# Attention logits by column-tiled matmuls, softmax in their layout, probabilities through DRAM

## The chip, the cores and the metric

The kernel runs on one core of one Trainium2 chip. The metric is the device time of one execution in microseconds (us). The engines are called PE (TensorE), DVE (VectorE), ACT (ScalarE), POOL (GpSimd) and SP (SyncE, which issues all DMAs here). The "span" of a profile runs from the first to the last instruction of a core and is some 2 us shorter than the device time.

## The reference

One layer on x of 2048 x 512 in bf16: layernorm, then the sum of x, a local attention and a gated feed-forward network.

```python
# attention: 32 heads of 16; query s sees keys s, s-2, ..., s-14
logits = jnp.einsum("bhsd,bhswd->bhsw", q, kg) * scale      # 8 keys per query and head
logits = jnp.where(mask[None, None, :, :], logits, -1e9)
attn = softmax(logits, axis=-1)
o = jnp.einsum("bhsw,bhswd->bhsd", attn, vg)                # then @ wo
# feed-forward: 512 -> 1376 -> 512
h = gelu(xn @ w_gate) * (xn @ w_up);  ffn = h @ w_down
return x + attention(xn) + ffn
```

## The kernel before

The program is a graph of tasks. A list scheduler inside the kernel orders them on each engine from guessed durations and priorities, over four blocks of 512 tokens. Each block's attention is: Q, K, V matmuls; on DVE 8 products PROD = Q * shifted K (head dims on partitions); the sum over 16 dims of each head on PE; softmax on DVE and ACT; on DVE 8 products PVS of probabilities (PT) with shifted V (BS, loaded from a DRAM copy of V); the sum over keys on PE (called the PVS reduction); then the output matmuls, accumulated with those of the feed-forward network. In the profiles PS is PSUM, where matmuls leave their results; XIN is x as loaded, XN and xnT its normalized forms; GG (after gelu) and UU are the two feed-forward projections and HT their product; OT is the attention output; E is a selector of zeros and constants; wsrc is zeros for filler matmuls.

The logits used the products as the stationary operand, so that queries land on partitions:

```python
for jj in range(4):
    w = 2 * (3 - jj) + wq
    wp = wmap(w)
    for ti in range(4):
        col = 512 * lg[ti // 2].slot + (ti % 2) * 256 + wp * 32 + 8 * g
        ins = e.matmul(PS[:, col:col + 8],
                       lhsT=PROD[:, it.slot, jj, ti * 128:(ti + 1) * 128],
                       rhs=E8[:, :], start=True, stop=True)   # 16 of these per task, 32 tasks
# ... softmax over [128 queries, 2 tiles x 8 keys x 32 heads] ...
ins = e.transpose(PSB[:, c0:c0 + 128], PB[:, ...], ident[:, :])        # "tpp", 4 per task, 8 tasks
e.activation(out=PT[:, ...], in_=PSB[...], func=ACTF.Identity)         # "evp", 8 in all
```

The sum over keys was column-tiled already: four matmuls with a 32-column selector, side by side in the array.

```python
for half in range(2):
    for d4 in range(4):
        ins = e.matmul(PS[32 * d4:32 * d4 + 32, 512 * it.slot:512 * it.slot + 512],
                       lhsT=E4[:, :], rhs=PVS[:, itp.slot, half, d4, :],
                       start=(half == 0), stop=(half == 1), tile_position=(0, 32 * d4))
```

Of the kernel before, what the change touches and what calls it, by code (L numbers as in the profile page):

```python
# [69 lines left out]

class Item:
    _n = 0

    def __init__(self, name, pool=None, stream=None, slot=None, psum=False):
        self.name = name
        self.pool = pool
        self.stream = stream
        self.slot = slot
        self.psum = psum or (pool is not None and pool.psum)
        self.tasks = []  # L80
        self.nleft = 0
        self.w_all = None
        self.w_part = {}
        self.r_all = []
        self.r_part = {}
        self.eng_last = {}
        self.alloc_task = None
        self.prev_tasks = []
        Item._n += 1
        self.uid = Item._n  # L90
# [37 lines left out]
class Graph:  # L128
# [117 lines left out]
    def schedule(self, params=None, prior=None):  # L246
# [38 lines left out]
        def res_time(t):  # L285
# [5 lines left out]
            for its in need.values():  # L291
# [4 lines left out]
                for it in its:  # L296
                    cnt[it.stream] = cnt.get(it.stream, 0) + 1
                for st, c in cnt.items():
                    q = pool.quotas.get(st)
                    if q is not None and pool.in_use.get(st, 0) + c > q:  # L300
                        return False, 0.0
                fr = sorted(pool.free, key=lambda x: (x[0], x[1]))
# [3 lines left out]
        def drop(t):  # L306
# [10 lines left out]
            for it in t.items:  # L317
                it.nleft -= 1
                it.tasks.remove(t)
                if it.nleft == 0 and it.pool is not None and it.slot is not None:  # L320
                    avail = max([x.done for x in it.tasks] + [0.0])
                    it.pool.free.append((avail, it.slot, it))
                    it.pool.in_use[it.stream] -= 1
            return 1

        while nsched < ntot:
# [73 lines left out]
            for it in t.items:  # L400
                if it.pool is not None and it.slot is None:
                    pool = it.pool
                    fr = min(pool.free, key=lambda x: (x[0], x[1]))
                    pool.free.remove(fr)
                    it.slot = fr[1]
                    pool.in_use[it.stream] = pool.in_use.get(it.stream, 0) + 1
                    it.alloc_task = t
                    it.prev_tasks = [pt for pt in fr[2].tasks if pt is not t] if fr[2] is not None else []
                    if fr[2] is not None:
                        for pt in fr[2].tasks:  # L410
                            if pt is not t:
                                t.deps.add(pt)
# [35 lines left out]
            for it in t.items:  # L448
                it.nleft -= 1
                if it.nleft == 0 and it.pool is not None:  # L450
                    avail = max(x.done for x in it.tasks)
                    it.pool.free.append((avail, it.slot, it))
                    it.pool.in_use[it.stream] -= 1
# [177 lines left out]
def bass_parallel_sum__sliding_local_dilated__glu_gated_geglu__prompt_kernel(nc, A_x, A_wqkv, A_wo, B_x, B_w_gate, B_w_up, B_w_down, out, dbg=None, cfg=None):  # L631
# [4 lines left out]
    NPROD = cfg.get("NPROD", 3)  # L636
    NMS = cfg.get("NMS", 3)
# [4 lines left out]
    NEXPB = cfg.get("NEXPB", 4)  # L642
    NDE = cfg.get("NDE", 8 // NEXPB)
    NPB = cfg.get("NPB", 2)
# [20 lines left out]
    CHAIN_SHIFT = cfg.get("CHAIN_SHIFT", [0, 0, 0, 0])  # L665
# [10 lines left out]
    with contextlib.ExitStack() as es:  # L676
# [5 lines left out]
        Wqkv = sb("Wqkv", [128, 4, 1024], BF)  # L682
        WV = sb("WV", [128, 4, 512], BF)
# [4 lines left out]
        xnT = sb("xnT", [128, 4, S], BF)  # L688
# [3 lines left out]
        E8 = sb("E8", [128, 8], BF)  # L692
        E8f = sb("E8f", [128, 8], F32)
        E4 = sb("E4", [128, 32], BF)
        E4f = sb("E4f", [128, 32], F32)
        mask = sb("mask", [128, 512], F32)
# [10 lines left out]
        ms = sb("ms", [128, NMS, 3, 64], F32)  # L707
# [4 lines left out]
        DE = sb("DE", [128, NDE, 512], F32)  # L712
        PB = sb("PB", [128, NPB, 512], BF)
        PT = sb("PT", [128, NPT, 2, 512], BF)
# [10 lines left out]
        PSB = PS.bitcast(BF)  # L725
        VD = nc.dram_tensor("vt_scratch", (512, PITCH), BF, kind="Internal")
# [8 lines left out]
        P_xn = Pool("xn", NXN)  # L735
        P_qt = Pool("qt", NQT)
# [19 lines left out]
        I_xnT = Item("xnT")  # L756
# [18 lines left out]
        I_wv = Item("WV")  # L775
        I_VD = Item("VD")
        I_out = Item("out")

        def wmap(w):
            return (w % 2) * 4 + w // 2  # L780
# [14 lines left out]
            out=E8f[:, :], in_=E8f[:, :], pattern=[[-16, 8]], compare_op=ALU.is_ge, fill=0.0, base=0,  # L795
            channel_multiplier=1), rd=[I_E8f], wr=[I_E8f], prio=PC2)
        G.task("pool", "c_e8c", 0.25, lambda e: e.affine_select(
            out=E8f[:, :], in_=E8f[:, :], pattern=[[16, 8]], compare_op=ALU.is_ge, fill=0.0, base=15,
# [13 lines left out]
        G.task("pool", "c_mask0", 0.7, lambda e: e.memset(mask[:, :], 0.0), wr=[I_mask], prio=PC2)  # L812
        for w in range(1, 8):
            def mk(w=w):
                wp = wmap(w)
                return lambda e: e.affine_select(
                    out=mask[:, wp * 32:(wp + 1) * 32], in_=mask[:, wp * 32:(wp + 1) * 32],
                    pattern=[[0, 32]], compare_op=ALU.is_ge, fill=-1.0e9, base=-2 * w, channel_multiplier=1)
            G.task("pool", "c_mask%d" % w, 0.3, mk(), rd=[I_mask], wr=[I_mask], prio=PC2 + 10)
# [20 lines left out]
        for i, nm in enumerate(("q", "k")):  # L840
# [5 lines left out]
        it_wvraw = Item("wvraw", P_ot, "ot")  # L846
        G.task("sp", "ld_wv", 0, lambda e: e.dma_start(
            OT[:, it_wvraw.slot, :, :], A_wqkv[:, 1024:1536].rearrange("(k p) n -> p k n", p=128)),
            wr=[it_wvraw], prio=-898, nbytes=512 * 1024)
        permv_tasks = []  # L850
        for kt in range(4):
            def mk(kt=kt):
                return lambda e: e.activation(
                    out=WV[:, kt, :].rearrange("q (d h) -> q d h", d=16),
                    in_=OT[:, it_wvraw.slot, kt, :].rearrange("q (h d) -> q d h", d=16), func=ACTF.Identity)
            permv_tasks.append(G.task("act", "permv%d" % kt, 1.0, mk(), rd=[it_wvraw], wr=[(I_wv, kt)],
                                      prio=13))
# [27 lines left out]
        XINI = []  # L885
        for p in range(NP):
# [98 lines left out]
            def mk_ev(p=p, it=it_tp):  # L985
                return lambda e: e.activation(  # L986
                    out=xnT[:, :, 256 * p:256 * p + 256],
                    in_=PSB[:, 1024 * it.slot:1024 * it.slot + 1024].rearrange("q (k c) -> q k c", k=4),
                    func=ACTF.Identity)
            t_evx = G.task("act", "evx%d" % p, d_act(1024), mk_ev(), rd=[it_tp], wr=[(I_xnT, p)], prio=base + 6)  # L990
            if p == 1:
                for t_pv in permv_tasks:
                    G.order_after(t_pv, t_evx)

        QTI = []
        exp_pairs_per_batch = NP // NEXPB
        for b in range(NB):
# [7 lines left out]
            for hf in range(nh):  # L1005
                xparts = [(I_xnT, 2 * b), (I_xnT, 2 * b + 1)] if nh == 1 else [(I_xnT, 2 * b + hf)]
                hb = base + (10 * hf if nh > 1 else 0)
                for which in range(3):
                    for g in range(4):
                        it_mm = Item("mm%d_%d_%d_%d" % (b, which, g, hf), P_ps, "qkv")  # L1010

                        def mk_mm(which=which, g=g, it=it_mm, c0=c0b + hf * HWD, HWD=HWD):
                            def f(e):
                                ins = None
                                for kt in range(4):
                                    if which < 2:
                                        lhsT = Wqkv[:, kt, which * 512 + g * 128:which * 512 + (g + 1) * 128]
                                    else:
                                        lhsT = WV[:, kt, g * 128:(g + 1) * 128]
                                    ins = e.matmul(PS[:, 512 * it.slot:512 * it.slot + HWD], lhsT=lhsT,  # L1020
                                                   rhs=xnT[:, kt, c0:c0 + HWD], start=(kt == 0), stop=(kt == 3))
# [3 lines left out]
                               rd=xparts + [(I_wq, "qk"[which]) if which < 2 else I_wv],  # L1025
# [17 lines left out]
                        else:  # L1043
# [7 lines left out]
                            def mk_s(g=g, it=it_vt[g][hf], c0=c0b + hf * HWD, HWD=HWD):  # L1051
                                return lambda e: e.dma_start(
                                    bass.AP(VD, g * 128 * PITCH + 16 + c0, [[PITCH, 128], [1, HWD]]),
# [4 lines left out]
            it_lg = [Item("lg%d_%d" % (b, h), P_ps, "lg") for h in range(2)]  # L1058
            for g in range(4):
                for wq in range(2):  # L1060
                    it_pr = Item("pr%d_%d_%d" % (b, wq, g), P_prod, "p")

# [11 lines left out]
                    def mk_r(wq=wq, g=g, it=it_pr, lg=it_lg):  # L1074
                        def f(e):
                            ins = None
                            for jj in range(4):
                                w = 2 * (3 - jj) + wq
                                wp = wmap(w)
                                for ti in range(4):  # L1080
                                    col = 512 * lg[ti // 2].slot + (ti % 2) * 256 + wp * 32 + 8 * g
                                    ins = e.matmul(PS[:, col:col + 8],  # L1082
                                                   lhsT=PROD[:, it.slot, jj, ti * 128:(ti + 1) * 128],
                                                   rhs=E8[:, :], start=True, stop=True)
                            return ins
                        return f
                    G.task("pe", "er%d_%d_%d" % (b, wq, g), d_mm(8, 16) + 0.06, mk_r(),
                           rd=[it_pr, I_E8], wr=[(it_lg[0], (wq, g)), (it_lg[1], (wq, g))], prio=base + 5, mode="f",
                           util=0.06)

            it_pt = Item("pt%d" % b, P_pt, "pt")
            for h2 in range(2):
                P = 2 * b + h2
                lg = it_lg[h2]
                batch = P // exp_pairs_per_batch
                it_de = Item("de%d" % P, P_de, "de")
                it_pb = Item("pb%d" % P, P_pb, "pb")
                it_ms = Item("ms%d" % P, P_ms, "ms")

                def lgv(lg=lg):  # L1100
# [318 lines left out]
```

## Time and profile before

The median was 214.04 us when the prediction was made, and 213.5 us in the groups of runs below.

| | PE | DVE | ACT |
|---|---|---|---|
| busy, us | 204.6 | 148.2 | 115.2 |
| share of the span | 97% | 70% | 54% |

The slices and the chain of waits are in the prediction. In the chain a piece "0.86 PE ... x4" is four matmuls of 512 columns issued 0.216 us apart.

### The profile page before, as it was taken

Reading aid. Unit: us, or ns where it says so; the run is one execution under the profiler, and the core shown is the slowest. Engines: PE = TensorE matmul, PEld = TensorE weight load, DVE = VectorE, ACT = ScalarE, POOL = GpSimd, SP = SyncE. Lnnn points to the kernel's source line nnn. Section 1 sums busy time; section 2 is a strip of 40 time slices with the busy share of each in tenths; the row PEclk is TensorE's granted clock in tenths of the full one; section 3 lists DMA queues with packets and bytes.
Section 4 is the critical chain, followed back from the end, with each engine's and each line's share of the span. In section 5 each row is a group of like instructions: output and inputs, shape, how many; then the busy total and the mean of one; then the engine's idle time right before and its main releaser. Section 6 shows DMA issues by size and latency. Waiting matters only on the chain.

```text
span 211.4 us, 3916 instructions
## 1 busy us (share of the span) xinstructions
PE 204.6 (97%) x1578; PEld 103.3 (49%) x1578; DVE 148.2 (70%) x239; ACT 115.2 (54%) x190; POOL 12.8 (6%) x44
## 2 busy tenths in 40 slices
PE   7799999999999999999999999999999999998994
PEld 2345565454444664544444654444445554443483
DVE  4508999999998597699822687698531887797121
ACT  2398767987810169976720149877400459848000
POOL 6701010010013000000000000000000000000000
PEclk9999999999999999999999999999999999999999
DMA  5999969023059610012012349140013258040021
GB/s 168 378 394 362 241 162 247 1 56 98 25 171 232 180 45 0 0 37 68 0 40 62 101 142 224 36 100 3 0 50 99 58 170 216 11 100 0 28 87 37
DMA packets 23777, 23.40 MB, mean 111 GB/s; under 512 B 2672, under 2 KB 22736, under 8 KB 23760
## 3 DMA queue, kind: packets, MB, share of 16 engines
q1 hardware_dynamic: 23760, 23.16, 38.4%
q8 instruction: 12, 0.20, 0.4%
q14 instruction: 5, 0.04, 0.1%
HBM read 18.94 MB, written 4.21 MB: 109 GB/s over the span
## 4 chain that ended last, share of the span: by engine, by line
PE 87%; DVE 7%; ACT 2%; DMA 1%; issue 1%; POOL 0%; ACTq 0%; DVEq 0%; POOLq 0%
PE PS L1242 32%; PE PS L1020 20%; PE PS L1289 18%; PE PS L1302 7%; PE PS L1082 6%; DVE PVS L1196 4%; PE PS L1211 3%; PE PS L978 2%; DVE st L907 1%; DMA XIN<-in_A_x_dram 1%; PE PS L1164 1%; DVE XN L965 1%; ACT PT L1173 1%; ACT xnT L986 0%; DVE HT L1264 0%
## 5 line engine op out<-in xcount | busy, mean ns | idle before, releaser
L1064 DVE TENSOR_TENSOR PROD<-QT,KT 128x2048 bf16<-128x2048 bf16 x32 | 37.3, 1219 | 11.5 <-ACT KT L1038 11.5
L1242 PE MATMUL PS<-xnT,Wu 128*128 128x512 bf16 (+1 forms) x176 | 45.2, 379 | 0.0
L1242 PE MATMUL PS<-xnT,Wg 128*128 128x512 bf16 (+1 forms) x176 | 45.1, 379 | 0.0
L1289 PE MATMUL PS<-Wd,HT 128*128 128x512 bf16 (+3 forms) x198 | 41.0, 356 | 0.2 <-ACT OT L1222 0.2
L1196 DVE TENSOR_TENSOR PVS<-BS,PT 128x2048 bf16<-128x2048 bf16 x32 | 37.0, 1220 | 3.6 <-ACT PT L1173 3.5
L1332 DVE TENSOR_TENSOR OB<-PS,XR 128x512 bf16<-128x512 f32 (+1 forms) x18 | 11.3, 630 | 31.9 <-PE PS L1302 31.8
L1020 PE MATMUL PS<-xnT,Wqkv 128*128 128x512 bf16 x128 | 30.3, 379 | 0.3 <-ACT xnT L986 0.3
L1252 ACT ACTIVATE GG<-PS 128x512 bf16<-128x512 f32 (+1 forms) x44 | 26.6, 604 | 6.4 <-PE PS L1242 6.1
L1259 ACT ACTIVATE UU<-PS 128x512 bf16<-128x512 f32 (+1 forms) x44 | 26.6, 604 | 4.6 <-PE PS L1242 4.4
L1289 PEld LDWEIGHTS PS<-Wd,HT 128*128 128x128 bf16 (+1 forms) x198 | 19.2, 98 | 19.1 <-ACT OT L1222 0.6
L1045 ACT ACTIVATE VT<-PS 128x512 bf16<-128x512 f32 x16 | 9.6, 598 | 34.4 <-PE PS L1020 34.4
L1242 PEld LDWEIGHTS PS<-xnT,Wu 128*128 128x128 bf16 (+1 forms) x176 | 16.9, 100 | 18.7 <-ACT QT L1031 0.4
L1242 PEld LDWEIGHTS PS<-xnT,Wg 128*128 128x128 bf16 (+1 forms) x176 | 17.0, 100 | 18.1
L1020 PEld LDWEIGHTS PS<-xnT,Wqkv 128*128 128x128 bf16 x128 | 11.9, 98 | 15.9 <-ACT KT L1038 0.8
L1038 ACT ACTIVATE KT<-PS 128x512 bf16<-128x512 f32 x16 | 9.6, 598 | 18.5 <-PE PS L1020 18.5
L1264 DVE TENSOR_TENSOR HT<-GG,UU 128x512 bf16<-128x512 bf16 (+1 forms) x44 | 16.8, 420 | 2.2 <-ACT UU L1259 2.2
L1082 PEld LDWEIGHTS PS<-E,PROD 128*128 128x128 bf16 x512 | 15.8, 96 | 4.5
L1302 PE MATMUL PS<-Wo,OT 128*128 128x512 bf16 (+1 forms) x72 | 16.8, 354 | 0.0
L1082 PE MATMUL PS<-E,PROD 128*128 128x8 bf16 x512 | 15.8, 166 | 0.0
L1020 PE MATMUL PS<-xnT,WV 128*128 128x512 bf16 x64 | 15.6, 378 | 0.0
L907 DVE BATCH_NORM_STATS2 st<-XIN 128x6 f32<-128x512 bf16 x16 | 10.7, 686 | 2.8 <-DMA XIN<-in_A_x_dram 2.8
L986 ACT ACTIVATE xnT<-PS 128x1024 bf16<-128x1024 bf16 x8 | 8.2, 1020 | 6.8 <-PE PS L978 6.8
(57 smaller groups left out, 147.1 us busy)
## 6 DMA issues: line engine op xcount, KB each, us to landing
BS<-vt_scratch SPq DMA_DIRECT2D x64, 128.5 KB, 3.4
XR<-in_A_x_dram SPq DMA_DIRECT2D x16, 128.0 KB, 2.2
vt_scratch<-VT SPq DMA_DIRECT2D x16, 128.0 KB, 1.7
XIN<-in_A_x_dram SPq DMA_DIRECT2D x7, 256.0 KB, 3.3
out_dram<-OB SPq DMA_DIRECT2D x14, 128.0 KB, 2.0
Wg<-in_B_w_gate_dram SPq DMA_DIRECT2D x1, 1376.0 KB, 9.5
Wu<-in_B_w_up_dram SPq DMA_DIRECT2D x1, 1376.0 KB, 12.5
Wd<-in_B_w_down_dram SPq DMA_DIRECT2D x1, 1280.0 KB, 9.8
```

Source lines behind the costliest of these rows:

```text
L907: return lambda e: e.bn_stats(out=st[:, t, :], in_=XIN[:, it.slot, t2, :])
L1020: ins = e.matmul(PS[:, 512 * it.slot:512 * it.slot + HWD], lhsT=lhsT, rhs=xnT[:, kt, c0:c0 + HWD], start=(kt == 0), stop=(kt == 3))
L1064: return lambda e: e.tensor_tensor(out=PROD[:, it.slot, :, :], in0=bass.AP(QT, (itq.slot * 4 + g) * 512, [[NQT * 4 * 512, 128], [0, 4], [1 ...
L1082: ins = e.matmul(PS[:, col:col + 8], lhsT=PROD[:, it.slot, jj, ti * 128:(ti + 1) * 128], rhs=E8[:, :], start=True, stop=True)
L1196: return lambda e: e.tensor_tensor(out=PVS[:, ito.slot, half, :, :], in0=BS[:, it.slot, :, o:o + 512], in1=bass.AP(PT, (itp.slot * 2 + hal ...
L1242: ins = e.matmul(PS[0:M, 512 * it.slot:512 * it.slot + 512], lhsT=Wx[:, kt, j * 128:j * 128 + M], rhs=xnT[:, kt, c0b:c0b + 512], start=(kt ...
L1252: return lambda e: e.activation(out=GG[0:M, ito.slot, :], in_=PS[0:M, 512 * it.slot:512 * it.slot + 512], func=ACTF.Gelu_apprx_tanh)
L1259: return lambda e: e.activation(out=UU[0:M, ito.slot, :], in_=PS[0:M, 512 * it.slot:512 * it.slot + 512], func=ACTF.Identity)
L1264: return lambda e: e.tensor_tensor(out=HT[0:M, ito.slot, j, :], in0=GG[0:M, ig.slot, :], in1=UU[0:M, iu.slot, :], op=ALU.mult)
L1289: ins = e.matmul(PS[:, 512 * it.slot:512 * it.slot + CW], lhsT=HT[0:K, ith.slot, j, ti * 128:(ti + 1) * 128], rhs=Wd[0:K, j, c0:c1], start ...
L1302: ins = e.matmul(PS[:, 512 * it.slot:512 * it.slot + CW], lhsT=OT[:, ito.slot, dq, ti * 128:(ti + 1) * 128], rhs=Wo[:, dq, c0:c1], start=F ...
L1332: return lambda e: e.tensor_tensor(out=OB[:, ito.slot, 0:CW], in0=PS[:, 512 * it.slot:512 * it.slot + CW], in1=XR[:, itx.slot, c0:c1], op= ...
```

## The change

The intent is to let PE stream the products through a small stationary selector, four query tiles at once, and not to load 512 blocks of products as weights for results of 8 columns. Logits then have heads on partitions, softmax runs in that layout, and the probabilities change to the layout of PVS by a store to DRAM and a load, which costs PE and ACT nothing. With it go other changes: V's permutation moves into the addresses of its store, so that WV need not be permuted on ACT; attention of later blocks gets a higher priority (CHAIN_SHIFT); xnT becomes three rotating buffers; PROD has four buffers for three. The core of the diff:

```diff
-    CHAIN_SHIFT = cfg.get("CHAIN_SHIFT", [0, 0, 0, 0])
+    CHAIN_SHIFT = cfg.get("CHAIN_SHIFT", [0, 300, 600, 900])
 ... (pools, buffers, mask, pairs of PSUM banks)
-                            for jj in range(4):
-                                ...
-                                    ins = e.matmul(PS[:, col:col + 8],
-                                                   lhsT=PROD[:, it.slot, jj, ti * 128:(ti + 1) * 128],
-                                                   rhs=E8[:, :], start=True, stop=True)
+                        for wq in range(2):
+                            for sj in range(4):
+                                ins = e.matmul(
+                                    PS[32 * sj:32 * sj + 32, 512 * (lg.slot + wq):512 * (lg.slot + wq) + 512],
+                                    lhsT=E8[:, 24 - 8 * g:56 - 8 * g],
+                                    rhs=PROD[:, prs[wq].slot, :, sj * 128:(sj + 1) * 128],
+                                    start=(g == 0), stop=(g == 3), tile_position=(0, 32 * sj))
 ... (softmax: the same steps, one of 1024 columns for two of 512)
-                G.task("pe", "tpp%d" % P, ...)      # transposes of the probabilities
-                G.task("act", "evp%d" % P, ...)     # and their eviction
+            for sj in range(4):                     # four stores ...
+                        bass.AP(PD, b * 128 * 1024 + sj * 256, [[1024, 32], [32 * 1024, 4], [1, 256]]),
+                        PB[32 * sj:32 * sj + 32, itp.slot, :].rearrange("q (j c) -> q j c", j=4))
+                    PT[:, it.slot, :], bass.AP(PD, b * 128 * 1024, [[1024, 128], [1, 1024]]))   # ... and a load
```

## The prediction

> **What bounds the kernel now.** I read the busy row and the 40 slices first. The slices show that TensorE (PE) is covered from the third slice to the 37th at full clock, while VectorE (DVE) and ScalarE (ACT) have holes.
>
> ```profile
> PE 204.6 (97%) x1578; PEld 103.3 (49%) x1578; DVE 148.2 (70%) x239; ACT 115.2 (54%) x190; POOL 12.8 (6%) x44
> PE   7799999999999999999999999999999999998994
> PEclk9999999999999999999999999999999999999999
> ```
>
> Busy TensorE time overlaps itself, because ends are modelled. I therefore read next the chain of waits in order of time, whose pieces on PE do not overlap. First the shares by line, from the page:
>
> ```profile
> PE 87%; DVE 7%; ACT 2%; DMA 1%; issue 1%; POOL 0%; ACTq 0%; DVEq 0%; POOLq 0%
> PE PS L1242 32%; PE PS L1020 20%; PE PS L1289 18%; PE PS L1302 7%; PE PS L1082 6%; DVE PVS L1196 4%; PE PS L1211 3%; PE PS L978 2%; DVE st L907 1%; DMA XIN<-in_A_x_dram 1%; PE PS L1164 1%; DVE XN L965 1%; ACT PT L1173 1%; ACT xnT L986 0%; DVE HT L1264 0%
> ```
>
> Then pieces of the chain (start, length, what):
>
> ```profile
> 10.93 7.08 PE PS L1020 x32
> 18.01 0.86 PE PS L1242 x4
> 18.88 0.38 PE PS L1082 x16
> ...
> 50.18 0.98 PE PS L1211 x16
> ...
> 71.34 1.18 PE PS L1082 x48
> ...
> 134.20 0.86 PE PS L1242 x4
> 135.06 0.22 PE PS L1164 x4
> ...
> 181.24 0.24 PE PS L1164 x4
> ```
>
> From 10.93 us to 181.5 us the chain is PE work laid end to end: four 512-column matmuls take 0.86 us, or 0.216 us each. After 181.5 us the chain leaves PE for the probabilities and PVS of the last block. That looks as if 13.6 us (181.5 to 195.1) were latency. The timeline of PE there says otherwise:
>
> ```profile
> 191.24 1.03 PE L1242 MATMUL PS<-xnT,Wu 128*96 128x512 bf16 x4
> 192.71 1.05 PE L1211 MATMUL PS<-PVS,E 128*32 128x512 bf16 x16 [0.44 <-ACT UU L1259]
> 193.69 1.25 PE L1362 MATMUL PS<-wsrc 128*128 128x512 bf16 x5
> 195.10 1.25 PE L1289 MATMUL PS<-Wd,HT 128*128 128x512 bf16 x5 [0.16 <-ACT OT L1222]
> ```
>
> PE still does feed-forward matmuls there until 192.1 us. Of the 3.0 us to 195.1 only 0.98 us is needed work (L1211); the L1362 fillers compute nothing. So about 2 us of the tail is lost, not 13.6. The kernel is a 10.9 us head, then about 184 us of needed PE issue time with 2 us lost near its end, 13.3 us of final accumulations, and about 3 us of output. **What leaves PE's stream shortens the time one for one, unless a new wait opens a hole in it.**
>
> **What the Trainium skill says.** "TensorE: Matmul & The Clock Gate", section Back-to-back issue gap, gives about 25 ns as the floor for 1 to 64 columns and N/2.4 + 2.5 ns for larger N. The trace agrees: 0.38 us for 16 matmuls of 8 columns is 24 ns each, and 512 columns take 216 ns. The old logits thus pay 16 issues and 16 weight loads for results of 8 columns.
>
> "TensorEngine Tiling (Array Packing)", section Key Properties, says that different tiles run weight loads and matmuls in parallel, and that a change of tiling mode drains TensorE. L1211 is already such a 128x32 matmul: 16 of them take 0.98 us, where four rounds of 0.216 are 0.86. So four do run at once, and a visit costs about 0.11 us extra.
>
> "SBUF — State Buffer", section Door 1, speaks of 16-byte lines, with a penalty for each access that crosses to a new line. The trace fits: the strided sum over SBUF takes 1038 ns for 512 elements (L1140), the same reduction from PSUM 685 ns (L1122).
>
> "DMA: Bandwidth & Descriptors", section Two DMAs through the same engine are not ordered, requires a wait for the first DMA's completion before a dependent one is issued. So the new path is two full trips in series. This trace has 128 KB stores to DRAM landing in 1.7 us, and loads of 128 to 256 KB in 2.2 to 3.4 us.
>
> **The change part by part.**
>
> Removed on PE: 32 logit tasks of 16 matmuls, at 0.38 to 0.39 us: 12.4 us. Also 8 transposes of probabilities (L1164) at 0.22: 1.8 us. Sum 14.2 us, all in the saturated stretch.
>
> Added on PE: 16 logit tasks of 8 column-tiled 512-column matmuls (four query tiles side by side, two PSUM banks, accumulated over the four head groups). In the order of the changed program they come as one visit of 16 and 14 of 8. By L1211's measure a visit of 8 costs 2 x 0.216 + 0.11 = 0.545 us; so 14 x 0.545 + 0.98 = 8.6 us. **Net on PE: minus 5.6 us.** All other matmul counts are unchanged in the order, apart from one more warm-up filler; the head stays bound by x, layernorm and the first transposes.
>
> ACT loses the permutation of WV (4.3 us) and the eviction of transposed probabilities (4.7 us), and about 0.5 us as four exponentials of 1024 columns replace eight of 512. ACT is not the bound: worth nothing directly.
>
> DVE: the softmax instructions now cost 8.0 + 4.9 + 4.5 + 4.5 + 3.8 + 1.0 + 0.7 + 0.7 = 28.1 us. The new ones per block: max, subtract and scale at about 1.2 us (twice 0.68 less one fixed part), sum about 2.0, reciprocal about 1.0, so four times 6.6 plus a small mask = 26.6 us. DVE is 1.5 us lighter, but in longer pieces. I expect PROD and PVS to keep their 1.22 us: the inner run of PVS becomes 128 elements, still contiguous bf16.
>
> Probabilities: before, a transpose of 0.22 and an eviction of 0.6 us. After, four stores issued at about 0.4 us, 1.7 us to land, one load of about 2.3 us: some 5.5 us from PB to PT, so 4 us more latency per block. The changed priorities move attention of later blocks ahead of feed-forward work to pay for this. In the new order the last block's second PVS reduction is followed by 13 feed-forward groups, so the roundtrip is out of the tail there. What stays at the end is the eviction and product of the last feed-forward tile, about 1.4 us from last matmul to first accumulation, against the 2 us lost now. Gain: 0.5 us.
>
> Do holes open in blocks 0 and 1? I walked the new order by hand with these durations. In block 0 the last logits end near 32.7 us, PB is ready near 42.5, PT near 48.4, and four PVS later (53 us) the first PVS reduction can start; PE arrives at 54.4. The second reduction is ready at 58.3, PE there at 58.5. That is tight, no hole. In block 1, counting from the end of block 0's accumulations, PB is ready at 16.5 us, PT at 22.0, DVE is free at 22.6, and the first reduction is ready at 27.2 while PE arrives at 26.9. The second must wait for four more PVS and two HT, 5.4 us, while PE has 4.4 us of other work: about 1 us. Block 2 has nearly 2 us of slack and block 3 more. I put 1.3 us on holes, with an uncertainty of 1.5 us.
>
> Sum: 214.04 - 5.6 - 0.5 + 1.3 = 209.2; I shade it to **209.0 us**, as the order is evidently laid out so that PE has other work near each wait.
>
> **The rivals.**
>
> First, DVE and the roundtrip become the bound in the first half. For it: DVE is busy 37.9 of 44 us between 11 and 55 us and 37.7 of 45 in the next stretch, and SyncE issues in order, so a store that waits for PB holds later loads. Against it: DVE's total falls, its second half is light (22.2 of 36.5 us from 145 to 181.5), and attention of block 0 had 4 us to spare before the accumulations. It would give back 3 to 6 us: 211 to 214.
>
> Second, no holes at all and a better tail: PE's saving comes through whole and the lost 2 us of the tail shrink by 1. For it: the kernel before has no PE hole above 0.5 us between 11 and 192 us, though its waits are similar. It would give 207.2 to 208.
>
> Third, column-tiled logits cost more than L1211's measure (each visit drains twice, or the strided reading of PROD is slower). At 0.8 us per visit instead of 0.545 the saving falls by 3.8 us: 212 to 213. Against it: L1211 has the same shape, contraction and stationary width.
>
> Fourth, the tail really was 13.6 us of latency and vanishes: 200 or less. Against it: the PE timeline above.
>
> **Range and chances.** The PE arithmetic alone gives 208; holes of 0 to 4 us lie on top, and 0.5 to 1 us may come from the tail. So 8 in 10 between 207.0 and 211.8. The 2% line is at 209.76, little above my centre: faster 0.60, within 2% 0.38, slower 0.02.
>
> **What would show it.** The column-tiled logits should fill about 8.6 us of the chain in pieces of 0.54 us; the line of probability transposes is gone; PVS stays at 1.22 us; the strided sum is near 2.0 us for 1024 elements; PT arrives about 5.5 us after PB. PE idle before the PVS reductions should total 0 to 3 us, mostly in blocks 0 and 1. The prediction is wrong if those waits exceed 4 us, if a logit visit costs over 0.7 us, if PVS falls out of its fast mode (8 us more on DVE for each 0.25 us), or if the span falls below 204 us.

## The result

The changed kernel took 210.09 us (median of 4; 210.00 to 210.33) against 213.74 us for the kernel before in the same group (213.40 to 214.10). The ratio of the fast runs is 0.9831, with a 95% interval from 0.9813 to 0.9849: 1.7% faster, within 2%. Ratios here and below are the mean time of one kernel's fast runs over that of the other's of the same rounds, so not quite the ratio of the medians quoted. The forecast range held; the centre of 209.0 was 1.1 us too low. Of the classes, the one given 0.60 (faster by more than 2%) did not come; "within 2%" had 0.38.

Busy times and slices of the changed kernel:

```profile
PE 200.5 (96%) x1142; PEld 90.6 (43%) x1163; DVE 147.9 (71%) x219; ACT 109.4 (53%) x174; POOL 11.4 (5%) x38
...
PE   7999999999989999999999999999999999999994
```

PE still covers nearly the whole span. (Of 1163 matmuls 1142 have a record; the count of weight loads is whole.) One slice has an 8, near 58 us. The chain of waits of the changed kernel, in the same columns as in the prediction:

```profile
26.05 0.55 PE PS L1083 x8
26.60 3.57 PE PS L1237 x16
...
104.64 0.98 PE PS L1206 x16
105.62 2.70 PE PS L1237 x12
...
190.82 0.60 ACT UU L1254
191.42 0.02 issue
191.45 0.43 DVE HT L1259
191.88 0.14 issue
192.01 2.54 PE PS L1284 x11
```

L1083 is the new logits line, L1206 the PVS reduction, L1237 the feed-forward line. A logit visit takes 0.55 us, as forecast. But look at what follows it: sixteen matmuls of 512 columns should take 16 x 0.216 = 3.46 us and take 3.57. The same holds after a PVS reduction, which is column-tiled too: twelve should take 2.59 and take 2.70. So **each visit also costs about 0.1 us after it**. The kernel before had the same 0.1 us after its PVS reductions (eight visits, unchanged: sixteen matmuls take 3.56), and only about 0.02 us after its old logits, which were not tiled (0.88 for 0.86). From its chain:

```profile
18.88 0.38 PE PS L1082 x16
19.26 0.88 PE PS L1242 x4
...
50.18 0.98 PE PS L1211 x16
51.16 3.56 PE PS L1020 x16
```

The chain goes by modelled ends. By starts the 0.1 us stands ahead of the visit and not behind it (this one starts at 25.98 us, where 25.88 was due); the sum is the same.

The final accumulations begin at 192.01 us against 195.10. From there on both kernels are equal (13.3 us to the last DVE step). All of the 3.1 us of span are gained before.

The timelines of PE where the 8 stands, of SP (issue of DMAs) ahead of it, and of DVE, in the changed kernel:

```profile
57.57 1.03 PE L1237 MATMUL PS<-xnT,Wg 128*128 128x512 bf16 x4
58.43 0.61 PE L986 MATMUL PS<-ident,XN 128*128 128x128 bf16 x8
59.98 1.05 PE L1206 MATMUL PS<-PVS,E 128*32 128x512 bf16 x16 [0.94 <-DVE PVS L1187]
```

```profile
43.10 0.78 SPq L1154 DMA_DIRECT2D pt_scratch<-PB  x2
43.98 0.40 SPq L907 DMA_DIRECT2D XIN<-in_A_x_dram  x1
44.42 0.96 SPq L1154 DMA_DIRECT2D pt_scratch<-PB  x2
47.40 0.34 SPq L1161 DMA_DIRECT2D PT<-pt_scratch  x1
```

```profile
41.79 1.23 DVE L1146 TENSOR_TENSOR PB<-DE,ms 128x1024 bf16<-128x1024 f32 x1
...
50.07 6.90 DVE L1187 TENSOR_TENSOR PVS<-BS,PT 128x2048 bf16<-128x2048 bf16 x6 [1.01 <-DMA PT<-pt_scratch]
```

PE waits 0.94 us for the last PVS products of block 0. The first began at 50.07 us, when PT landed; PB had been ready at 43.0. That is 7 us for the roundtrip, not the 5.5 forecast. A 256 KB load of x stands among the four stores, and PT's load is issued only when the last store has landed. It is the only large hole; block 1, where the prediction put 1 us, has none before its PVS reductions.

The softmax rows of the changed kernel, from the groups of instructions by form (busy us and mean ns after the count):

```profile
L1187 DVE TENSOR_TENSOR PVS<-BS,PT 128x2048 bf16<-128x2048 bf16 x32 | 37.3, 1217 | 3.6 <-DMA PT<-pt_scratch 2.6 <-PE PS L1206 1.0
L1138 DVE TENSOR_REDUCE ms<-DE 128x128 f32<-128x1024 f32 x4 | 7.7, 1914 | 2.5 <-ACT DE L1133 2.5
L1122 DVE TENSOR_REDUCE ms<-PS 128x128 f32<-128x1024 f32 x4 | 4.9, 1222 | 0.3 <-PE PS L1083 0.3
```

PVS kept its 1.22 us and the strided sum over SBUF takes 1.91 us, both as forecast. All softmax instructions on DVE come to 26.5 us, against 26.6 forecast.

My theory after this: PE's stream sets the time; each of the 16 logit visits costs about 0.21 us for going into column-tiled mode and coming back, of which the prediction counted half; and the late PT of block 0 costs about 1 us. The rivals: that the 0.1 us are an artefact of modelled ends; that DVE's load makes the hole; that ACT's lighter load was part of the gain.

### The profile page after: what moved, and what is told of

Same layout as the page of the kernel before. It is cut to its first block, busy times and chain, and to the rows that moved or that the text cites. A ratio compares the mean times of both kernels' runs of the same rounds, so it can differ in the third digit from the quotient of the medians.

```text
span 208.3 us, 3060 instructions
## 1 busy us (share of the span) xinstructions
PE 200.5 (96%) x1142; PEld 90.6 (43%) x1163; DVE 147.9 (71%) x219; ACT 109.4 (53%) x174; POOL 11.4 (5%) x38
## 4 chain that ended last, share of the span: by engine, by line
PE 90%; DVE 5%; issue 1%; DMA 1%; ACT 1%; POOL 0%; POOLq 0%; DVEq 0%
PE PS L1237 36%; PE PS L1021 19%; PE PS L1284 18%; PE PS L1297 7%; PE PS L1206 4%; PE PS L1083 3%; DVE st L915 2%; PE PS L986 1%; DVE PROD L1068 1%; DVE PVS L1187 1%; DMA XIN<-in_A_x_dram 1%; DVE XN L973 1%; ACT UU L1254 1%; PE PS L854 1%; POOL sq L930 0%
## 5 line engine op out<-in xcount | busy, mean ns | idle before, releaser
L1237 PE MATMUL PS<-xnT,Wu 128*128 128x512 bf16 (+1 forms) x170 | 44.4, 379 | 0.6 <-issue 0.3
L1237 PE MATMUL PS<-xnT,Wg 128*128 128x512 bf16 (+1 forms) x172 | 44.7, 379 | 0.3 <-ACT UU L1254 0.2
L1021 PE MATMUL PS<-xnT,Wqkv 128*128 128x512 bf16 x187 | 43.6, 379 | 0.4 <-DVE PROD L1068 0.2
L1247 ACT ACTIVATE GG<-PS 128x512 bf16<-128x512 f32 (+1 forms) x44 | 26.5, 603 | 12.1 <-PE PS L1237 10.7
L1254 ACT ACTIVATE UU<-PS 128x512 bf16<-128x512 f32 (+1 forms) x44 | 26.5, 602 | 6.0 <-PE PS L1237 5.8
L1021 PEld LDWEIGHTS PS<-xnT,Wqkv 128*128 128x128 bf16 x192 | 18.0, 98 | 24.5 <-issue 2.1
L1259 DVE TENSOR_TENSOR HT<-GG,UU 128x512 bf16<-128x512 bf16 (+1 forms) x44 | 17.2, 417 | 13.3 <-ACT UU L1254 13.2
L1237 PEld LDWEIGHTS PS<-xnT,Wu 128*128 128x128 bf16 (+1 forms) x176 | 17.1, 100 | 21.7 <-ACT GG L1247 2.1
L1237 PEld LDWEIGHTS PS<-xnT,Wg 128*128 128x128 bf16 (+1 forms) x176 | 16.9, 100 | 21.2 <-issue 2.5
L1032 ACT ACTIVATE QT<-PS 128x512 bf16<-128x512 f32 x16 | 9.3, 595 | 27.7 <-PE PS L1021 27.7
L1217 ACT ACTIVATE OT<-PS 128x512 bf16<-128x512 f32 x16 | 8.7, 594 | 16.4 <-PE PS L1206 16.4
L994 ACT ACTIVATE xnT<-PS 128x1024 bf16<-128x1024 bf16 x8 | 8.2, 1024 | 8.6 <-PE PS L986 8.6
L1083 PE MATMUL PS<-PROD,E 128*32 128x512 bf16 x128 | 9.8, 384 | 0.2 <-PE PS L1083 0.2
## 6 DMA issues: line engine op xcount, KB each, us to landing
Wg<-in_B_w_gate_dram SPq DMA_DIRECT2D x1, 1376.0 KB, 10.5
```

Source lines behind the costliest of these rows:

```text
L1021: ins = e.matmul(PS[:, 512 * it.slot:512 * it.slot + HWD], lhsT=lhsT, rhs=xnT[:, itx.slot, kt, c0:c0 + HWD], start=(kt == 0), stop=(kt == 3))
L1083: ins = e.matmul(PS[32 * sj:32 * sj + 32, 512 * (lg.slot + wq):512 * (lg.slot + wq) + 512], lhsT=E8[:, 24 - 8 * g:56 - 8 * g], rhs=PROD[:, ...
L1237: ins = e.matmul(PS[0:M, 512 * it.slot:512 * it.slot + 512], lhsT=Wx[:, kt, j * 128:j * 128 + M], rhs=xnT[:, itx.slot, kt, :], start=(kt = ...
L1247: return lambda e: e.activation(out=GG[0:M, ito.slot, :], in_=PS[0:M, 512 * it.slot:512 * it.slot + 512], func=ACTF.Gelu_apprx_tanh)
L1254: return lambda e: e.activation(out=UU[0:M, ito.slot, :], in_=PS[0:M, 512 * it.slot:512 * it.slot + 512], func=ACTF.Identity)
L1259: return lambda e: e.tensor_tensor(out=HT[0:M, ito.slot, j, :], in0=GG[0:M, ig.slot, :], in1=UU[0:M, iu.slot, :], op=ALU.mult)
```

## The experiments

Twelve kernels ran, in three groups, each group on one chip. Except for `pairs`, `pairs_xin`, `before_shift`, `after_noshift` and `noshift_pt_early`, which let the scheduler plan anew, the changed kernel's order on each engine is kept apart from what is named.

### Control

> The changed kernel once more, as the control of this group of runs: 210.1 us, within 0.3, and the same hole of about 0.9 us on TensorE before the second PVS reduction of block 0.

Measured 210.20 us (209.99 to 210.40), with the same hole of 0.9 us. The differences of this group below are taken to it.

### What a visit costs

Zeros are multiplied ahead of the first logits of each block; the logits overwrite the result. `full()` is a 128-column matmul of 256 columns, `tiled()` a round of four column-tiled ones.

```diff
 # trips_grouped                        # trips_alternate
+for rep in range(4): full()           +for rep in range(4):
+for rep in range(4): tiled()          +    tiled()
                                       +    full()
```

> Before the first logits of each block, 4 full-width matmuls of 256 columns and then 4 rounds of 4 column-tiled ones, all on zeros and overwritten by the logits (result stays right). No additional change of mode. 4 x (4 x 0.107 + 4 x 0.107) = 3.4 us slower than the changed kernel, 213.5 us.

> The same matmuls as in the grouped run, but alternating: one tiled round, one full matmul, four times. That is 16 additional trips into column-tiled mode and back. Two-way theory (0.11 in, 0.10 out): 16 x 0.21 = 3.4 us slower than the grouped run. One-way theory: 1.8 us slower. If a change of mode costs nothing and the 0.1 us are an artefact of modelled ends: equal to the grouped run within 0.3 us.

Measured 213.39 us grouped and 216.93 us alternating; both results correct. The same matmuls in another order cost 3.5 us more (3.4 by the ratios), for 16 trips: **0.21 to 0.22 us a trip**. The timeline of PE, first grouped, then alternating:

```profile
20.34 0.60 PE L1084 MATMUL PS<-wsrc 128*128 128x256 bf16 x4
20.87 0.62 PE L1088 MATMUL PS<-wsrc 128*32 128x256 bf16 x16
```

```profile
20.14 0.29 PE L1088 MATMUL PS<-wsrc 128*32 128x256 bf16 x4
20.37 0.28 PE L1084 MATMUL PS<-wsrc 128*128 128x256 bf16 x1
20.58 0.29 PE L1088 MATMUL PS<-wsrc 128*32 128x256 bf16 x4
```

Alternating, one tiled round and one full matmul repeat every 0.44 us (20.14 to 20.58), where two streams of 256 columns need 0.21. From one start to the next pass 0.23 us and 0.21 us, for 0.107 us of stream each. So the cost lies on both ways, and the one-way theory and the artefact fall.

What is it: a drain of the array, or a weight load that is not hidden behind the matmuls of the other mode? The changed kernel's own trace answers in part. Weight loads (PEld) and matmuls around the visit at 26 us:

```profile
25.98 0.12 PEld L1083 LDWEIGHTS PS<-PROD,E 128*32 128x32 bf16 x8 [0.42 <-DVE PROD L1068]
26.53 0.55 PEld L1237 LDWEIGHTS PS<-xnT,Wg 128*128 128x128 bf16 x4 [0.42 <-ACT GG L1247]
27.19 0.75 PEld L1237 LDWEIGHTS PS<-xnT,Wu 128*128 128x128 bf16 x4
...
25.98 0.62 PE L1083 MATMUL PS<-PROD,E 128*32 128x512 bf16 x8
26.53 1.04 PE L1237 MATMUL PS<-xnT,Wg 128*128 128x512 bf16 x4
27.41 0.81 PE L1237 MATMUL PS<-xnT,Wu 128*128 128x512 bf16 x3
```

Within a mode the weights begin to load 0.22 us ahead of their first matmul (27.19 and 27.41). At both changes of mode they begin with it (25.98 and 26.53), and one load lasts about 0.1 us, as much as each way costs. So the load is not hidden at a change; whether a drain holds it back, these runs do not tell.

```diff
-for wq in range(2):
-    for sj in range(4):
+for wq, rep, sj in [(q, r, j) for q in range(2) for r in range(2) for j in range(4)]:
         ins = e.matmul(... column-tiled logits, as in the change ...)
```

> Each visit issues its 8 column-tiled logit matmuls twice (softmax then sees doubled logits, so the result is wrong on purpose); visits and order stay. If four tiles run at once at L1211's rate also with the strided reading of PROD: 16 x 2 x 0.216 = 6.9 us slower than the changed kernel, 217.0 us. If the strided reading slows the stream: 9 us or more slower.

Measured 216.87 us, 6.7 us more than the control of the first group (210.20 us, on another chip; the kernel before agrees between the groups within 0.1 us). That is 0.42 us for 8 more matmuls per visit: four tiles do run at once, also on PROD's strided rows. The variable part of a visit was priced rightly; the fixed part was not.

```diff
-G.task("pe", "er%d_%d" % (b, g), 0.46, mk_r(), rd=prs + ...)             # 16 tasks, one head group each
+if g % 2 != 1: continue
+G.task("pe", "er%d_%d" % (b, g), 0.44 * 2 + 0.02, mk_r(), rd=prs_of[g - 1] + prs_of[g] + ...)   # 8 tasks
```

> The logits of two head groups are computed in one visit to column-tiled mode: 8 visits of 16 matmuls instead of 16 of 8; the order is planned anew. Two-way theory (a visit costs about 0.11 us on the way in and 0.10 on the way out, the part that the prediction left out): 8 x 0.21 = 1.7 us faster than the changed kernel, 208.4 us, if no new hole opens. One-way theory (0.11 us on entry only): 0.9 us faster, 209.2 us. If waiting for four products instead of two opens holes: 210 us or more, with TensorE idle before the logits.

Measured 208.46 us (208.37 to 208.92), ratio to before 0.9756 (0.9733 to 0.9779), correct. Eight trips fewer give 1.7 us, the two-way figure. That it fits so well is in part luck, because the order is new: the wait before block 0's second reduction is 0.38 us here and not 0.94, a wait of 0.5 us before logits has come in (66.1 us), and the first Q, K and V matmuls begin 0.4 us later (11.36 us). The clean measure of a trip is the pair of trips kernels. `pairs` is the fastest correct kernel, 0.8% ahead of the changed one (0.9756 / 0.9833 = 0.992).

### What the roundtrip costs

```diff
 SP order in block 0:  store, store, [load of x], store, store, load of PT
                    -> store, store, store, store, load of PT, [load of x]
```

> Every engine keeps its order except SyncE, which issues one load of x after block 0's probability load instead of between the stores that it waits for. Roundtrip theory (the hole of 0.9 us before the second PVS reduction of block 0 comes from the late PT): PT lands 0.9 to 1.3 us earlier, the hole goes, 0.6 to 1.0 us faster than the changed kernel, about 209.2 us. DVE theory (VectorE's amount of work between 50 and 62 us makes the hole): no change, 210.1 us within 0.2. Mixed: a hole of equal length moves to another place, no change in time.

Measured 209.09 us (208.94 to 209.16), correct: 1.1 us faster by moving one DMA issue. SP and PE of this run:

```profile
43.10 1.77 SPq L1154 DMA_DIRECT2D pt_scratch<-PB  x4
46.24 0.34 SPq L1161 DMA_DIRECT2D PT<-pt_scratch  x1
```

```profile
58.35 0.61 PE L986 MATMUL PS<-ident,XN 128*128 128x128 bf16 x8
58.98 1.05 PE L1206 MATMUL PS<-PVS,E 128*32 128x512 bf16 x16
```

PT's load is issued at 46.24 us, 1.2 us earlier than in the changed kernel, and the reduction follows the transposes with 0.63 us between starts where it was 1.55. The DVE theory falls: DVE had the same work, and its PVS products began at 49.06 us instead of 50.07.

```diff
-PT[:, it.slot, :] <- PD (after the four stores have landed)
+PT[:, it.slot, :] <- A_x (no wait for the stores; issued ahead of them, all four blocks)
```

> Wrong result on purpose: PT is filled from x instead of the stored probabilities, without waiting for the stores, and the load is issued ahead of them; the stores and every engine's order otherwise stay. So the roundtrip through DRAM costs no latency at all. Roundtrip theory: all waits for PT go, TensorE holes shrink from about 1.5 us to about 0.5, 1.0 us faster than the changed kernel, 209.1 us (208.8 to 209.4). DVE theory: no change, 210.1 us. If the roundtrip cost more than the holes that I see, below 208.5 us.

Measured 208.84 us, with a wrong result: 1.4 us faster than the control. This is the most that the roundtrip's latency costs the changed kernel, in all blocks (PVS no longer waits for softmax through PT either), and 1.1 us of it went with that one load of x.

> Both gains together: logits of two head groups per visit, and in SyncE's order block 0's four stores of probabilities and the load of PT ahead of two loads of x that stood among them. In the pairs run the two reductions of block 0 still found TensorE waiting for about 0.4 us, and PT was issued behind a load of x. If the gains add up: 0.5 to 1.1 us faster than the pairs run, 207.4 to 208.0 us. If the loads of x, now later, hold the next layernorm: 208.5 us or more.

Measured 209.47 us (209.10 to 209.64): 1.0 us slower than `pairs`, which ran in another group but against a kernel before that agrees within 0.1 us. The gains do not add up: this missed my first forecast and met the other. DVE in this run:

```profile
48.70 0.34 DVE L957 TENSOR_SCALAR XN<-XIN,mv 128x512 bf16<-128x512 bf16 x1
51.25 0.69 DVE L915 BATCH_NORM_STATS2 st<-XIN 128x6 f32<-128x512 bf16 x1 [2.20 <-DMA XIN<-in_A_x_dram]
...
53.80 6.87 DVE L1194 TENSOR_TENSOR PVS<-BS,PT 128x2048 bf16<-128x2048 bf16 x6
```

In this plan a layernorm step stands on DVE ahead of PVS. With x loaded later DVE waits 2.2 us for x, and PVS starts at 53.80 us; in `pairs` it started at 52.79. DVE keeps its order, so it stood behind x although PT was on its way: I had moved the wrong load back.

### What the other parts are worth

```diff
 # in the kernel before, nothing else
-    CHAIN_SHIFT = cfg.get("CHAIN_SHIFT", [0, 0, 0, 0])
+    CHAIN_SHIFT = cfg.get("CHAIN_SHIFT", [0, 300, 600, 900])
```

> The kernel before with only the changed priorities (attention of blocks 1, 2 and 3 moved ahead by 300, 600 and 900); logits, softmax and probabilities as before. If the tail holds about 2 us of lost TensorE time and 1.4 stay in any case, 0.5 us faster than the kernel before: 213.2 us (212.8 to 213.6). If the 13.6 us of the chain's tail were latency, 205 us or less. If the priorities alone open holes, 214 us or more.

Measured 218.02 us (216.35 to 218.34), ratio 1.018 (1.0135 to 1.0225). My expectation of a small gain missed. The new priorities by themselves cost 4.4 us, 2.8 us in the run with a granted clock of 0.999 and some 4.5 in the three with 0.992. In the profiled run the chain of waits leaves PE at 25 us and goes through DVE for most of the time to 57 us, so they crowd DVE's busy first part; I did not test this reading.

```diff
 # in the changed kernel, nothing else
-    CHAIN_SHIFT = cfg.get("CHAIN_SHIFT", [0, 300, 600, 900])
+    CHAIN_SHIFT = cfg.get("CHAIN_SHIFT", [0, 0, 0, 0])
```

> The changed kernel without the changed priorities. The last block's probabilities then come about 5 us later after its last logits than in the kernel before, with less feed-forward work behind them. My theory: TensorE runs dry before the last PVS reductions, 2 to 5 us slower than the changed kernel, 212 to 215 us. Rival (TensorE has enough feed-forward work left there): 210.1 us within 0.5.

Measured 220.41 us (220.20 to 221.17), ratio 1.0314: 10.3 us slower than the changed kernel. The direction was expected, the size was not. PE near the end:

```profile
187.73 1.03 PE L1237 MATMUL PS<-xnT,Wu 128*96 128x512 bf16 x4
188.81 2.54 PE L1347 MATMUL PS<-wsrc 128*128 128x512 bf16 x11
195.32 1.08 PE L1206 MATMUL PS<-PVS,E 128*32 128x512 bf16 x16 [3.97 <-DVE PVS L1187]
196.33 3.17 PE L1347 MATMUL PS<-wsrc 128*128 128x512 bf16 x7
```

The feed-forward work ends at 188.6 us and the final accumulations start at 202.2. Of these 13.6 us only 2.1 are needed work (two reductions), so 11.5 us are lost, against 1.4 in the changed kernel; the difference is the whole loss. The granted clock is 0.992 over the run; it is 0.76 and then 0.50 in the 3.7 us after the empty stretch (195.3 to 199 us), where PE runs fillers beside one reduction.

> Wrong result on purpose: the changed kernel without the changed priorities, with PT filled from x ahead of the stores, so without the roundtrip. If the roundtrip at the tail is what makes the kernel without the changed priorities slow (220.4 us), the wait of 4 us before the last reductions goes, and with it the dip of the granted clock: 213 to 216 us. If the old priorities are bad for the new logits whatever the roundtrip: 219 us or more.

Measured 218.44 us in its three fast runs (218.36 to 218.47): 2.0 us less than 220.41. The roundtrip is thus a small part of that loss, and the time lies near my rival's figure. Most of the loss, by my reading, is in how the old priorities place block 3's attention with the new tasks: so late that after its last logits (176.5 us without the shift) only 14 feed-forward groups of 0.865 us are left, 12 us. In the fast profile of `after_noshift` the way from there to the final accumulations takes 25.7 us: softmax to 184.7, the roundtrip to 190.5, PVS to 199.7, reduction to 202.2. The roundtrip's 5.8 us gave back only 2.0, so another wait stands close behind it. Which one would come last I cannot show: the profile of this run fell in the slow state (clock 0.56, 361 us) and is not used.

```diff
 # 28 activations on zeros, each 0.42 us in the trace, at the places of the old permutation and evictions
+order["act"]: 6 before the first Q eviction, 6 before the first V eviction, 4 before each block's OT evictions
```

> 28 activations of 256 columns put back on ScalarE, near the places where the kernel before permuted WV and evicted the transposed probabilities; at about 0.35 us each 9.8 us, as much as the change took away there. The result stays right. If ScalarE's saving is worth nothing in itself: the changed kernel's time within 0.5 us, 209.8 to 210.6 us. If it was part of the gain: 211.5 us or more.

Measured 210.43 us (210.29 to 210.51), correct. ACT's busy time rose from 109.4 to 118.3 us, by more than the 5.8 us that the change had taken away, and the time by 0.2 us (0.4 by the ratios, 0.9851 to 0.9833, whose intervals overlap). ACT's saving is worth little or nothing here.

## Why the prediction was right, and what was mis-sized

1. **PE's stream sets the time.** Right. ACT's 9 us put back cost 0.2 to 0.4 us, trips on PE are paid in full (3.5 us for 16), and eight trips fewer gave 1.7 us.

2. **Removed from PE: 14.2 us.** Right to 0.4 us: the old visits also lengthened the next group by 0.02 us.

3. **Added to PE: 8.6 us at 0.545 us a visit.** The term that was mis-sized. Within the visit 0.55 us was right, and so was the concurrency (0.42 us for 8 matmuls). I had priced L1211 by its own length and not looked at the group behind it, where 0.1 us more is spent. The prediction also took the first two visits of block 1 for one of 16 matmuls in 0.98 us. They came as two (76.62 and 77.40 us, 0.78 and 0.55 us long), the second 0.17 us behind the end of the first. With 14 x (0.55 + 0.10) and 0.78 + 0.55 + 0.10 the added work is 10.5 us, and PE's net saving is 14.2 + 0.4 - 10.5 = 4.1 us, not 5.6. The third rival, that each visit is paid twice, was the one that came true, at 0.65 us a visit and not the 0.8 that I had tried for it.

4. **The tail gives 0.5 us.** Right: from the last feed-forward matmul to the first accumulation 1.4 us were forecast and measured (190.6 to 192.0), against 2.0 us lost before, and the fourth rival, a tail of pure latency, did not come. One reading was off: the 37th slice of the kernel before, counted as covered, has an 8; the lost 2 us lie there.

5. **Holes cost 1.3 us.** The sum came out (at most 1.4 us by `pt_early`), but by luck, because the place was wrong. Block 0 was called tight without a hole, and its second reduction waited 0.94 us, because PT came 7 us after PB and not 5.5: I had left out what the load of x among the stores does to the landing of the last one. Block 1, given 1 us, lost nothing visible.

6. **DVE and the roundtrip as the bound** (first rival). Not in this kernel. DVE's softmax fell by 1.6 us (1.5 forecast), though its busy time only by 0.3 (148.2 to 147.9). But `before_shift` and `pairs_xin` show how near it is: each puts DVE's waits in front.

The sum with the measured terms, from 213.6 us: minus 4.1, minus 0.5, plus 1.4 is 210.4 us, against 210.1 to 210.2 measured.

## What to carry to other kernels

Price a matmul mode by the whole trip: its own length and what the next group loses; if a trip is dear, put more work into each (two head groups per visit gave back 1.7 us, with a new order). A transfer through DRAM is cheap when the order keeps other work beside it: here 7 us of latency cost 1.4 us at most. One unrelated transfer among the stores made 1.1 us of that; but `pairs_xin` shows that moving such a transfer back can cost as much, when another engine waits for it. Priorities belong to the kernel that they were tuned with: the new ones lose 4.4 us in the old kernel, and the old ones lose 10.3 us in the new.

## What the Trainium skill lacked or had wrong

- "TensorEngine Tiling (Array Packing)", Key Properties, says that a change of tiling mode drains TensorE, and gives no cost. Here a trip into column-tiled mode and back costs 0.22 us (3.54 us for 16 trips), about half on each way.
- "TensorE: Matmul & The Clock Gate", Back-to-back issue gap, gives 131 ns per matmul of 512 columns in a real stream of weight loads and matmuls, and says that the isolated 216 ns over-count. Here the stream runs at 0.86 us for 4, which is 216 ns, through some 180 us. In this kernel the page's isolated formula is the right one.
- The same page, Measured speedup vs the span model, has column tiling alone for three tiles only. With four column tiles and 512 columns, 8 matmuls more per visit cost 0.42 us (6.7 us for 16 visits), against 8 x 0.216 = 1.7 us one after another: four at once.
- "DMA: Bandwidth & Descriptors", Two DMAs through the same engine are not ordered, demands the wait between a store and the load of the same data, without a figure for the whole trip. Here stores of 64 KB landed in 1.8 us and the dependent load of 256 KB in 2.6; with four issues of about 0.44 us, PB to PT took 7.0 us with a load of x in between, and that one load cost 1.1 us of the kernel's time.
- "SBUF — State Buffer", Door 1, gives the 16-byte lines but no cost for a strided fp32 reduction. Here 1914 ns for 1024 elements from SBUF, against 1222 ns for a strided reduction of the same size from PSUM (a maximum, not a sum). The operation is not the cause: in the kernel before the same maximum took 1046 ns for 512 elements from SBUF and 685 from PSUM.
